# Last two chunks of a chunked mLSTM: products in a bank of their own, scores moved up, output work in two parts

## The chip, the cores and the metric

One NeuronCore of a Trainium2 chip runs the whole program. The metric is device time in microseconds (us), the median of several executions; a profiled execution gives the trace. The engines are TensorE (PE, with its weight loads PEld), VectorE (DVE), ScalarE (ACT), GpSimd (POOL) and SyncE (SP, which issues transfers). PE writes its results to PSUM, which has eight banks; DVE and ACT read them there.

## What is computed

An mLSTM layer (4 batches, 8 heads, 768 steps, head size 40), then a soft mixture of 8 experts and a second mixture with 8 Sinkhorn iterations, all on 3072 rows of 320. The part that matters here is the mLSTM:

```python
C = f_stab * C + i_stab * outer(v_t, k_t)
n = f_stab * n + i_stab * k_t
h_tilde = C @ q_t
denom = max(abs(n . q_t), 1)
y_t = sigmoid(o_t) * h_tilde / denom
```

## The kernel before

The mLSTM is done in chunks of 128 steps, six for each batch, 24 in all (numbers 0 to 23). For a chunk i the kernel makes:

- **scores** (`s_p`, L401): products of the transposed k and q, all heads, into two banks of the pool `ps_s`, which has two in all. `s_d` (L408, DVE, two instructions W0 and W1) multiplies them by the decay matrix `dd` in place, and with that frees the banks.
- **state** (`st_p`, L413, into bank `ob`; `st_d`, L429): the state after this chunk.
- **own products** (`pv`, L439): weighted scores times v, 32 small matmuls into the columns `o_in` of bank `oa`.
- **state products** (`p_st`, L449): q times the state before the chunk, 16 small matmuls, half into the columns `o_st` of `oa`, half into `ob`.
- **output** (`y_d`, DVE): two L460 read `o_st` and scale it into `u`, L467 adds `o_in`, L470, L474 and L475 make the denominator, L477 multiplies by the output gate. `y_g` (L487) multiplies by 1/denominator, on POOL, for chunk 23 on DVE.

Two chunks behind, `x_p`/`x_a` transpose the output rows (L498, copied by ACT at L503), and for each group of four chunks `lg_p` (L521) makes logits, `lg_d` (L529, L534, DVE) their running maximum, `lg_e` (ACT) the exponentials, `lt_p` (L562) transposes them, `sl_p` (L593) and `sl_d` (L604, DVE, accumulator `sacc`) sum the slot inputs.

`step(i)` writes the work of one iteration out in the order of the string `ORDER`; the last two chunks (22 and 23) use `ORDER_L`. PE, ACT and SP keep the order written, for the last two steps DVE does too; instructions of different hand-ordered blocks can still be interleaved on DVE and ACT by the scheduler that builds the program. In `ORDER_L` the score step `S` of iteration i makes the scores of chunk i+1. So PE's order at the end is: state 22, own products 22, state products 22, scores 23, logits of group 4, transposes of chunk 20, own products 23, state products 23, `lt_p`, transposes of chunk 21.

Then the string `TAIL` (L890) finishes the attention: transposes of chunks 22 and 23 (`x22p`, `x23p`), slot sums of group 4 (`s4p`, `s4d`), the transposed combine weights of groups 0 to 3 (`0p` to `3p`, `c_p`, L798, with `0a`.. on ACT and `0d`.. on DVE), logits of the last group (`lp`, `ld`), the maximum over all (`mxp`, L841), `wk` (two 512-column matmuls of the identity into bank `oa`, whose results nobody reads), and `ftp`/`ftd` (L868, L878), which end in `siT`, the slot inputs. `siT` feeds `up(0)` (L924), the first of the eight experts of the first mixture. The second mixture (L1184 to L1222) follows. The weights of the first mixture are fetched by SP during the attention and while its experts run.

Of the kernel before, what the change touches and what calls it, by code (L numbers as in the profile page):

```python
# [9 lines left out]
F32 = mybir.dt.float32  # L10
# [5 lines left out]
ALU = mybir.AluOpType  # L16
# [5 lines left out]
def mlstm_moe_kernel(  # L22
# [16 lines left out]
    nc = tc.nc  # L39
    B, H, S, D = q.shape  # L40
    N, DM = out.shape
    E, _, F = m2_w1.shape
    NS = phi.shape[1]
    SPE = NS // E
    BH = B * H
    P = 128
    L = 128
    NCH = S // L
    NT = N // P
# [6 lines left out]
    D1 = D + 1  # L56
# [6 lines left out]
    NXR = 13  # L63
    NBIG = 3
    ORDER = "LF' PK STm R DV DK O KT KTa ST STd E0 E0a E0g V I Y QT QTa Yg S W0 W1 E1 E1a E1g LP LV X Xa LD G LA W SM IR"
    ORDER_L = "LF' PK STm R DV DK O ST STd V I S W0 W1 Y Yg LP LV X Xa LD G LA W"
    PB = [1, 2, 3]
    PD = 3
    MAN2 = "Activation SP".split()
# [52 lines left out]
    ps_e = actx.enter_context(tc.tile_pool(name="ps_e", bufs=PB[0], space=PSUM))  # L122
    ps_s = actx.enter_context(tc.tile_pool(name="ps_s", bufs=PB[1], space=PSUM))
# [1 line left out]
    ps_o = actx.enter_context(tc.tile_pool(name="ps_o", bufs=1, space=PSUM))  # L125

    oa, ob = (ps_o.tile([P, 512], F32, name=n) for n in ("oa", "ob"))
    o_in = oa[:, 0:H * D1].rearrange("p (h d) -> p h d", h=H)
    o_st = [t[:, H * D1:H * D1 + JP * D1].rearrange("p (j d) -> p j d", j=JP) for t in (oa, ob)]
    o_c = ob[:, 0:JP * D1].rearrange("p (j d) -> p j d", j=JP)  # L130

# [7 lines left out]
    def xs_(i, w=DM):  # L139
        return xr[:, i % NXR, 0:w]  # L140
# [208 lines left out]
    def k_p(i, a):  # L349

        pt = ps_t.tile([P, JP, L], F32, tag="t", name="ptk")
        for j in range(JP):
            nc.tensor.transpose(  # L353
                pt[:, j, :], kq[i % NQ][:, a, 2 * j:2 * j + 2, :].rearrange("p h d -> p (h d)"), ident,
            )
        tmp["k", a, i] = pt

    def k_a(i, a, eng=None):
        t = pre.tile([P, JP, L], F32, tag=f"T{a}", name=f"T{a}", bufs=2 + a)
        if eng is None:  # L360
            nc.scalar.copy(out=t, in_=tmp.pop(("k", a, i)))  # L361
        else:
            eng.tensor_copy(t, tmp.pop(("k", a, i)))
        Ts[i, a] = t

    dds = {}
# [11 lines left out]
    def e_a(i, hh):  # L378
        dd = pre.tile([P, 4, L], F32, tag="dd", name="dd", bufs=6)
        nc.scalar.activation(out=dd, in_=tmp.pop(("e", i, hh)), func=AF.Exp)  # L380
        dds[i, hh] = dd
# [51 lines left out]
    def pv(i):  # L433

        TH = L // 2
        for r in range(2):
            for j in range(JP):
                for a in range(2):
                    nc.tensor.matmul(  # L439
                        o_in[TH * a:TH * a + TH, 2 * j + r, :], dds[i, r][:, j, TH * a:TH * a + TH],  # L440
                        vz[i % NV][:, 2 * j + r, :], start=True, stop=True, tile_position=(0, TH * a),
                    )

# [7 lines left out]
                    start=True, stop=True, tile_position=(DP * r, 0),  # L451
                )

    def y_d(i):
        b, c = divmod(i, NCH)
        src = o_in
        if c:
            src = mid.tile([P, H, D1], F32, tag="u", name="u", bufs=1)
            for r in range(2):
                nc.vector.tensor_tensor(  # L460
                    out=src.rearrange("p (j r) d -> p r j d", r=2)[:, r], in0=o_st[r],
                    in1=eGt[:, c, b * H:(b + 1) * H].rearrange("p (j r) -> p r j", r=2)[:, r].unsqueeze(2).to_broadcast(
                        [P, JP, D1]
                    ),
                    op=ALU.mult,
                )
            nc.vector.tensor_tensor(out=src, in0=src, in1=o_in, op=ALU.add)  # L467
        nq = mid.tile([P, H, 1], F32, tag="nq", name="nq")

        nc.vector.tensor_scalar(  # L470
            out=nq.bitcast(I32), in0=src[:, :, D:D1].bitcast(I32), scalar1=0x7FFFFFFF, scalar2=None,
            op0=ALU.bitwise_and,
        )
        nc.vector.tensor_scalar(out=nq, in0=nq, scalar1=1.0, scalar2=2.0, op0=ALU.max, op1=ALU.mult)  # L474
        nc.vector.reciprocal(nq, nq)  # L475
        xs = xs_(i).rearrange("p (h d) -> p h d", h=H)
        nc.vector.scalar_tensor_tensor(  # L477
            out=xs, in0=xs, scalar=1.0, in1=src[:, :, 0:D], op0=ALU.add, op1=ALU.mult,
        )
        nqs[i] = nq  # L480
# [3 lines left out]
    def y_g(i):  # L484
        xs = xs_(i).rearrange("p (h d) -> p h d", h=H)
        eng = nc.gpsimd if i < NT - 1 else nc.vector
        eng.tensor_tensor(out=xs, in0=xs, in1=nqs.pop(i).to_broadcast([P, H, D]), op=ALU.mult)  # L487
# [161 lines left out]

    ahead_parts = ahead()  # L650

    def step(i):
        b, c = divmod(i, NCH)
        n, s1 = i + 2, i + 1
        T, S1 = n < NT, s1 < NT
        X = i >= 2
        gq, j = divmod(i - 2, 4)
        gq -= 1
        if gq < 0 or not X:
            j = 9  # L660
        C_ = c < NCH - 1
        nxt = b + 1 < B

        ops = dict(
            KT=lambda: T and k_p(n, 0), KTa=lambda: T and k_a(n, 0),
            QT=lambda: T and k_p(n, 1), QTa=lambda: T and k_a(n, 1),
            E0=lambda: T and e_p(n, 0), E0a=lambda: T and e_a(n, 0), E0g=lambda: T and e_g(n, 0),
            E1=lambda: T and e_p(n, 1), E1a=lambda: T and e_a(n, 1), E1g=lambda: T and e_g(n, 1),
            ST=lambda: C_ and st_p(i), STm=lambda: C_ and st_m(i), STd=lambda: C_ and st_d(i),
            S=lambda: S1 and s_p(s1), W0=lambda: S1 and s_d(s1, 0), W1=lambda: S1 and s_d(s1, 1),  # L670
            PK=lambda: T and pr_k(n),
            V=lambda: pv(i), I=lambda: c and p_st(i),
            X=lambda: X and x_p(i - 2), Xa=lambda: X and x_a(i - 2),
            Y=lambda: y_d(i), Yg=lambda: y_g(i),
            G=lambda: i in SIG and sig_o(*SIG[i]),
            IR=lambda: c in (1, 2) and nxt and init_R(b + 1, c - 1, nc.vector.tensor_copy),
            LP=lambda: j < 3 and (lg_p, lt_p, sl_p)[j](gq), LV=lambda: j == 1 and lt_v(gq),
            LD=lambda: j < 3 and (lg_d, lt_d, sl_d)[j](gq), LA=lambda: j < 2 and (lg_e, lt_a)[j](gq),
            LF=lambda: j == 1 and lt_f(gq),
            O=lambda: load_o(*LO[i]),  # L680
            R=lambda: i + 3 < NT and load_R(i + 3),
            W=lambda: load_w(islice(ahead_parts, WN[i])),
            SM=lambda: i == 2 and load_small(),
            DV=lambda: T and i and load_v(n),
            DK=lambda: i + 4 < NT and load_kq(i + 4),
        )
        for o in (ORDER if i < NT - 2 else ORDER_L).split():
            if o.endswith("'"):
                if last:
                    last[-1][o[:-1]]()  # L690
            elif i < NT:
                ops[o]()
        last[:] = [ops]

# [65 lines left out]
        step(i)  # L760
    man2d = tc.manual_schedule(engines={mybir.EngineType.DVE})
    man2d.__enter__()
    for i in range(NT - 2, NT + 1):
        step(i)
    man2d.__exit__(None, None, None)
    if man2:
        man2.__exit__(None, None, None)
# [64 lines left out]
                tile_position=(0, 64 * a),  # L832
            )

    cbk = [(ps_e, "e"), (ps_s, "s"), (ps_s, "s"), (oa, None)]
    rs = pb.tile([P, 1, NS], F32, name="rs", bufs=1)
    siT = pb.tile([P, 3, NS], F32, name="siT", bufs=1)

# [25 lines left out]
    def ft_p():  # L864
        ptf = ob

        pfs = ps_e.tile([P, 512], F32, tag="e", name="pfs")[:, 0:NS]
        nc.tensor.matmul(  # L868
            pfs, sacc[:, DM:DM + 1].to_broadcast([P, P]), foldw, start=True, stop=True,
        )  # L870
        fold_t(ptf, sacc, foldw)
        tmp["f"] = ptf, pfs
# [7 lines left out]
            op=ALU.mult,  # L880
        )

    wm = oa.rearrange("p (a l) -> p a l", a=4)

    def wk():

        for _ in range(2):
            nc.tensor.matmul(wm, ident16, ident16.unsqueeze(1).to_broadcast([P, 4, L]), start=True, stop=True)

    TAIL = "x22p x22a 0p s4p 0a x23p x23a s4d 1p 2p lp 1a wk ld la mxp ls tp mxd wk tv mbp 0d mbd mba sp lc fwd sd 3p ftp tq 1d te ftd 2a 3a 2d ltd lta ltf 3d"  # L890
    ops = dict(
        wk=wk, x22p=lambda: x_p(NT - 2), x22a=lambda: x_a(NT - 2), s4p=lambda: sl_p(gl - 1), s4d=lambda: sl_d(gl - 1),
        x23p=lambda: x_p(NT - 1), x23a=lambda: x_a(NT - 1), lp=lambda: lg_p(gl), ld=lambda: lg_d(gl),
        la=lambda: lg_a(gl, 1), lc=lambda: lg_a(gl, 0), ls=lambda: lg_s(gl),
        tp=lambda: lt_p(gl, (1,)), tq=lambda: lt_p(gl, (0,)), tv=lambda: lt_v(gl, 1), te=lambda: lt_v(gl, 0), mxp=mx_p, mxd=mx_d,
        mbp=mb_p, mbd=mb_d, mba=mb_a, fwd=fw_d, sp=lambda: sl_p(gl), sd=lambda: sl_d(gl), ftp=ft_p, ftd=ft_d,
        ltd=lambda: lt_d(gl), lta=lambda: lt_a(gl), ltf=lambda: lt_f(gl),
    )
# [6 lines left out]
    if man3:  # L905
        man3.__enter__()
    for o in TAIL.split():
        ops[o]()
# [444 lines left out]
    for n in range(1, NBLK):  # L1353
        e, tb = divmod(n, NB)
# [60 lines left out]
```

## Time and profile before

| | |
|---|---|
| median of 3 runs | 942.7 us (941.76 to 942.98) |
| profiled execution | 941.64 us |
| its span, first to last instruction | 939.9 us |
| mean granted PE clock | 0.998 of full speed |
| PE busy | 98% of the span |
| chain of work that ended last | PE 94%, DVE 4% |

The span is what the trace covers; 1.74 us of the execution lie around it. Attention fills the first 172 us or so, the first mixture ends near 207 us, the rest is the second mixture. A row of the timeline gives start, duration, engine, line, operation, output <- inputs and the count of merged instructions; behind it, in brackets, how long the engine had been idle and what released it.

### The profile page before, as it was taken

Reading aid. Unit: us, or ns where it says so; the run is one execution under the profiler, and the core shown is the slowest. Engines: PE = TensorE matmul, PEld = TensorE weight load, DVE = VectorE, ACT = ScalarE, POOL = GpSimd, SP = SyncE. Lnnn points to the kernel's source line nnn. Section 1 sums busy time; section 2 is a strip of 40 time slices with the busy share of each in tenths; the row PEclk is TensorE's granted clock in tenths of the full one; section 3 lists DMA queues with packets and bytes.
Section 4 is the critical chain, followed back from the end, with each engine's and each line's share of the span. In section 5 each row is a group of like instructions: output and inputs, shape, how many; then the busy total and the mean of one; then the engine's idle time right before and its main releaser. Section 6 shows DMA issues by size and latency. Waiting matters only on the chain.

```text
span 939.9 us, 18808 instructions
## 1 busy us (share of the span) xinstructions
PE 917.4 (98%) x7966; PEld 631.6 (67%) x7966; DVE 576.8 (61%) x1182; ACT 358.0 (38%) x699; POOL 85.8 (9%) x151
## 2 busy tenths in 40 slices
PE   5999999999999999999999999999999999999998
PEld 3888887436767666666666666666666666666665
DVE  6667677645889785664665557555745464545443
ACT  3555554335334334422442344243424242423221
POOL 3555453000000000000000000000000000000000
PEclk9999999999999999999999999999999999999999
DMA  9999999960011011010110001010100000000111
GB/s 204 159 159 191 195 179 278 335 195 1 1 57 32 26 57 56 26 32 1 57 56 1 30 28 57 1 57 1 57 2 1 1 1 1 1 1 33 46 43 50
DMA packets 129612, 63.65 MB, mean 68 GB/s; under 512 B 103544, under 2 KB 123288, under 8 KB 129528
## 3 DMA queue, kind: packets, MB, share of 16 engines
q1 hardware_dynamic: 128416, 61.87, 28.7%
q8 instruction: 62, 1.02, 0.5%
q10 hardware_dynamic: 1112, 0.59, 0.3%
q14 instruction: 22, 0.18, 0.1%
HBM read 58.07 MB, written 4.08 MB: 66 GB/s over the span
## 4 chain that ended last, share of the span: by engine, by line
PE 94%; DVE 4%; ACT 1%; issue 1%; POOL 0%; ACTq 0%; DVEq 0%; POOLq 0%
PE y L1207 22%; PE y L1206 22%; PE y L1205 22%; PE z L1184 9%; PE pss L401 3%; PE oa L439 3%; PE ptk L353 3%; PE oa L449 2%; PE pu L924 2%; PE pe L371 2%; PE ob L413 1%; PE pd L962 1%; PE pu L931 1%; PE ptx L498 1%; DVE hl L1188 1%
## 5 line engine op out<-in xcount | busy, mean ns | idle before, releaser
L1206 PE MATMUL y<-wx,hh 128*128 128x320 f16 x1344 | 401.6, 299 | 0.4 <-DVE wx L1042 0.4
L1205 PE MATMUL y<-wx,hh 128*128 128x320 f16 x1344 | 401.9, 299 | 0.0
L1207 PE MATMUL y<-wx,hl 128*128 128x320 f16 x1344 | 401.7, 299 | 0.0
L1187 ACT ACTIVATE hh<-z 128x512 f16<-128x512 f32 x384 | 209.3, 594 | 438.2 <-PE z L1184 437.7
L1188 DVE SCALAR_TENSOR_TENSOR hl<-z,hh 128x512 f16<-128x512 f32 x384 | 248.2, 684 | 52.8 <-ACT hh L1187 52.3
L1220 DVE SCALAR_TENSOR_TENSOR acc<-y,Ps,acc 128x320 f32<-128x320 f32 x168 | 92.3, 550 | 209.9 <-PE y L1207 209.5
L1205 PEld LDWEIGHTS <-hh 128*128 128x128 f16 x1536 | 150.3, 98 | 75.0 <-issue 2.0
L1206 PEld LDWEIGHTS <-hh 128*128 128x128 f16 x1536 | 150.2, 98 | 73.4
L1207 PEld LDWEIGHTS <-hl 128*128 128x128 f16 x1536 | 149.9, 98 | 61.1 <-DVE hl L1188 1.9
L1184 PE MATMUL z<-cst,sst 96*128 96x512 f16 x384 | 115.7, 379 | 2.2 <-DVE hl L1188 1.4
L1207 PE MATMUL y<-wh,hl 128*128 128x320 f16 x192 | 57.4, 299 | 0.3 <-DVE hl L1188 0.3
L1205 PE MATMUL y<-wh,hh 128*128 128x320 f16 x192 | 57.4, 299 | 0.0
L1206 PE MATMUL y<-wl,hh 128*128 128x320 f16 x192 | 57.3, 299 | 0.0
L1184 PEld LDWEIGHTS <-sst 96*128 96x128 f16 x384 | 37.2, 98 | 18.7 <-issue 2.9
L353 PE MATMUL ptk<-ident,kq 128*128 128x128 f32 x192 | 31.1, 289 | 9.3 <-POOL ident masks.py:199 9.3
L361 ACT COPY T<-ptk 128x512 f32<-128x512 f32 x46 | 26.9, 585 | 31.7 <-PE ptk L353 31.4
L380 ACT ACTIVATE dd<-pe 128x512 f32<-128x512 f32 x48 | 29.0, 604 | 23.8 <-PE pe L371 20.5
L408 DVE TENSOR_TENSOR dd<-pss,dd 128x512 f32<-128x512 f32 x48 | 30.2, 670 | 9.1 <-PE pss L401 9.1
L1011 POOL PARTITION_ALL_REDUCE mr<-mxs x8 | 2.9, 365 | 325.0 <-DVE mxs L1030 325.0
L385 POOL TENSOR_SCALAR_AFFINE_SELECT dd<-dd 128x512 f32<-128x512 f32 x48 | 32.2, 675 | 4.2 <-ACT dd L380 4.2
L1011 POOL PARTITION_ALL_REDUCE mr<-mx x8 | 3.0, 375 | 295.6 <-DVE mx L1000 277.8
L353 PEld LDWEIGHTS ptk<-ident,kq 128*128 128x128 f32 x192 | 22.5, 146 | 10.5 <-POOL ident masks.py:199 9.3
(236 smaller groups left out, 753.8 us busy)
## 6 DMA issues: line engine op xcount, KB each, us to landing
wa<-in_moe_w_dram SPq DMA_DIRECT2D x18, 512.0 KB
raw<-in_moe_w_dram SPq DMA_DIRECT2D x28, 320.0 KB
kq<-in_k_dram SPq DMA_DIRECT2D x24, 160.0 KB
kq<-in_q_dram SPq DMA_DIRECT2D x24, 160.0 KB
vz<-in_v_dram SPq DMA_DIRECT2D x24, 160.0 KB
xr<-in_o_gate_dram SPq DMA_DIRECT2D x24, 160.0 KB
wb<-in_moe_w_dram SPq DMA_DIRECT2D x6, 640.0 KB
out_dram<-acc SPq DMA_DIRECT2D x24, 160.0 KB
```

Of the source, the lines that this page charges most:

```text
L353: nc.tensor.transpose(pt[:, j, :], kq[i % NQ][:, a, 2 * j:2 * j + 2, :].rearrange("p h d -> p (h d)"), ident,)
L380: nc.scalar.activation(out=dd, in_=tmp.pop(("e", i, hh)), func=AF.Exp)
L385: nc.gpsimd.affine_select(out=dd, in_=dd, pattern=[[0, 4], [1, L]], compare_op=ALU.is_ge, fill=0.0, base=0, channel_multiplier=-1,)
L401: nc.tensor.matmul(ps[r][:, j, :], Ts[i, 0][rs_, j, :], Ts[i, 1][rs_, j, :], start=True, stop=True, tile_position=(DP * r, 0),)
L408: nc.vector.tensor_tensor(out=dds[i, r], in0=tmp["s", i][r], in1=dds[i, r], op=ALU.mult)
L1184: nc.tensor.matmul(z, Sst[e][:, kc * P:(kc + 1) * P], cst[:, tb * TB:(tb + 1) * TB], start=True, stop=True,)
L1187: nc.scalar.activation(out=hh[:, kc, :], in_=z, func=AF.Relu)
L1188: nc.vector.scalar_tensor_tensor(out=hl[:, kc, :], in0=z, scalar=0.0, in1=hh[:, kc, :], op0=ALU.max, op1=ALU.subtract)
L1205: nc.tensor.matmul(y, hh[:, kc, ts], wh[e][:, kc, :], start=(kc == 0), stop=False)
L1206: nc.tensor.matmul(y, hh[:, kc, ts], wl[e][:, kc, :], start=False, stop=False)
L1207: nc.tensor.matmul(y, hl[:, kc, ts], wh[e][:, kc, :], start=False, stop=(kc == KF - 1))
L1220: nc.vector.scalar_tensor_tensor(out=a, in0=y, scalar=Ps[:, i, e:e + 1], in1=a, op0=ALU.mult, op1=ALU.add)
```

## The change

The own products of chunk 23 go to a tile `oe` of the pool `ps_e` (one bank) in place of `oa`. `y_d` is cut into `y_u` (L460, L467) and `y_r` (the rest). The steps 22 and 23 are no longer run one after the other: a string `LAST` writes out both, `a` for step 22 and `b` for step 23. In it the scores of chunk 23 (`aS`) stand ahead of the own products of the chunk before (`aV`, counted from 0 as chunk 22), and the own products of chunk 23 (`bV`) ahead of the output work of chunk 22. In `TAIL`, `0p` moves behind `x23p`, `2p` moves behind `lp` into the place of the first of two `wk`, which goes. Group 0's transposed weights and group 3's swap banks (`oa` and `ps_e`), as do `pfs` and `wm`.

```diff
-    ORDER_L = "LF' PK STm R DV DK O ST STd V I S W0 W1 Y Yg LP LV X Xa LD G LA W"
+    LAST = "aSTm aW bW aST aSTd aS aV aI aW0 aW1 bV aYu aLP bI aYr aYg aLD aLA aX aXa bYu bLP bLV bX bXa bYr bYg bLD bLA bLF"
...
-    o_in = oa[:, 0:H * D1].rearrange("p (h d) -> p h d", h=H)
+    banks = {}
+
+    def o_in(i):
+
+        return banks.get(i, oa)[:, 0:H * D1].rearrange("p (h d) -> p h d", h=H)
+
...
-    def y_d(i):
+    us = {}
+
+    def y_u(i):
         b, c = divmod(i, NCH)
-        src = o_in
+        src = o_in(i)
...
-            nc.vector.tensor_tensor(out=src, in0=src, in1=o_in, op=ALU.add)
+            nc.vector.tensor_tensor(out=src, in0=src, in1=o_in(i), op=ALU.add)
+        us[i] = src
+
+    def y_r(i):
+        src = us.pop(i)
...
-            Y=lambda: y_d(i), Yg=lambda: y_g(i),
+            Y=lambda: (y_u(i), y_r(i)), Yu=lambda: y_u(i), Yr=lambda: y_r(i), Yg=lambda: y_g(i),
...
-    for i in range(NT - 2, NT + 1):
-        step(i)
+    banks[NT - 1] = ps_e.tile([P, 512], F32, tag="e", name="oe")
+    ends = dict(a=step_ops(NT - 2), b=step_ops(NT - 1))
+    for o in LAST.split():
+        ends[o[0]][o[1:]]()
...
-    cbk = [(ps_e, "e"), (ps_s, "s"), (ps_s, "s"), (oa, None)]
+    cbk = [(oa, None), (ps_s, "s"), (ps_s, "s"), (ps_e, "e")]
...
-        pfs = ps_e.tile([P, 512], F32, tag="e", name="pfs")[:, 0:NS]
+        pfs = oa[:, 0:NS]
...
-    wm = oa.rearrange("p (a l) -> p a l", a=4)
-
     def wk():
 
+        wm = ps_e.tile([P, 4, L], F32, tag="e", name="wm")
...
-    TAIL = "x22p x22a 0p s4p 0a x23p x23a s4d 1p 2p lp 1a wk ld la mxp ls tp mxd wk tv mbp 0d mbd mba sp lc fwd sd 3p ftp tq 1d te ftd 2a 3a 2d ltd lta ltf 3d"
+    TAIL = "x22p x22a s4p x23p x23a s4d 0p 1p 0a lp 1a 2p ld la mxp ls tp mxd wk tv mbp 0d mbd mba sp lc fwd sd 3p ftp tq 1d te ftd 2a 3a 2d ltd lta ltf 3d"
```

## Rows read from the trace of the kernel before

**Rows 1.** The page's first part: busy time and share of each engine.

```profile
PE 917.4 (98%) x7966; PEld 631.6 (67%) x7966; DVE 576.8 (61%) x1182; ACT 358.0 (38%) x699; POOL 85.8 (9%) x151
```

**Rows 2.** The chain that ended last, 156 to 163 us: start, us, what.

```profile
156.63 1.02 PE pss L401 x16
157.76 0.55 issue
158.31 0.68 DVE dd L408
158.99 0.48 DVE u L460 x2
159.49 0.51 DVE u L467
160.04 1.13 PE oa L439 x32
...
162.24 0.56 DVE u L460 x2
```

**Rows 3.** PE's timeline at the end of the attention.

```profile
153.94 0.67 PE L413 MATMUL ob<-vz,kp 128*64 128x41 f32 x16
154.43 1.18 PE L439 MATMUL oa<-vz,dd 128*64 128x41 f32 x32
155.54 0.30 PE L449 MATMUL oa<-C,T 64*128 64x41 f32 x1
...
156.46 1.14 PE L401 MATMUL pss<-T,T 64*128 64x128 f32 x16
157.53 0.86 PE L521 MATMUL pl<-xT,phi_sb 112*32 112x128 f32 x24
158.32 0.54 PE L498 MATMUL ptx<-ident,xr 128*112 128x128 f32 x3
160.04 1.13 PE L439 MATMUL oa<-vz,dd 128*64 128x41 f32 x32 [1.18 <-DVE u L467]
161.10 0.30 PE L449 MATMUL oa<-C,T 64*128 64x41 f32 x1
...
163.06 0.60 PE L798 MATMUL ptc<-ident,ct_all 128*32 128x128 f32 x4
...
167.12 0.61 PE L888 MATMUL oa<-ident 128*128 128x512 f16 x2
```

**Rows 4.** DVE's timeline of the same stretch.

```profile
153.65 1.25 DVE L408 TENSOR_TENSOR dd<-pss,dd 128x512 f32<-128x512 f32 x2
...
158.91 0.32 DVE L460 TENSOR_TENSOR u<-oa,eGt 128x164 f32<-128x164 f32 x1
...
161.24 0.21 DVE L534 TENSOR_SCALAR nmx<-gm,nmx 128x1 f32<-128x1 f32 x1
162.22 0.33 DVE L460 TENSOR_TENSOR u<-oa,eGt 128x164 f32<-128x164 f32 x1 [0.77 <-PE ob L449]
...
164.37 0.49 DVE L487 TENSOR_TENSOR xr<-xr,nq 128x320 f32<-128x320 f32 x1
...
164.98 0.54 DVE L604 SCALAR_TENSOR_TENSOR sacc<-sacc,sc,pq 128x321 f32<-128x321 f32 x1
```

**Rows 5.** PE's timeline: entry to the experts, and the second mixture's first weights.

```profile
172.41 1.07 PE L924 MATMUL pu<-wa,siT 128*32 128x256 f32 x16 [0.33 <-DVE siT L878]
...
202.63 1.07 PE L924 MATMUL pu<-big,soT 128*32 128x256 f32 x16
```

**Rows 6.** Busy time by stretch: stretch, length, engines (count), granted clock, DMA share, GB/s.

```profile
18.00:20.00 2.00, 0.42 (x2) 0.00 (x1) 0.82 (x4) 0.60 (x1) 0.69 (x2) 0.95 1.01 177
20.00:22.00 2.00, 2.00 (x15) 1.62 (x16) 0.00 (x0) 0.60 (x1) 1.38 (x3) 0.50 0.94 304
...
194.00:196.00 2.00, 2.00 (x30) 0.89 (x30) 0.66 (x2) 1.37 (x3) 0.00 (x0) 1.00 0.38 105
```

**Rows 7.** PE's timeline: scores while the clock was low.

```profile
20.38 2.08 PE L401 MATMUL pss<-T,T 64*128 64x128 f32 x16
```

More of the change, by code (lines that the diff above doesn't have):

```diff
@@ L435, in pv @@
         TH = L // 2
+        o = o_in(i)
         for r in range(2):
@@ L439, in pv @@
                     nc.tensor.matmul(
-                        o_in[TH * a:TH * a + TH, 2 * j + r, :], dds[i, r][:, j, TH * a:TH * a + TH],
+                        o[TH * a:TH * a + TH, 2 * j + r, :], dds[i, r][:, j, TH * a:TH * a + TH],
                         vz[i % NV][:, 2 * j + r, :], start=True, stop=True, tile_position=(0, TH * a),
@@ L650, in mlstm_moe_kernel, with step_ops @@
     ahead_parts = ahead()
-    def step(i):
+    def step_ops(i):
         b, c = divmod(i, NCH)
@@ L662, in step @@
         nxt = b + 1 < B
-        ops = dict(
+        return dict(
             KT=lambda: T and k_p(n, 0), KTa=lambda: T and k_a(n, 0),
@@ L686, in step @@
         )
-        for o in (ORDER if i < NT - 2 else ORDER_L).split():
+    def step(i):
+        ops = step_ops(i)
+        for o in ORDER.split():
             if o.endswith("'"):
@@ L690, in step @@
                     last[-1][o[:-1]]()
-            elif i < NT:
+            else:
                 ops[o]()
```

## The prediction

> **What bounds the kernel now.** I read the page's busy shares first: PE is busy for 98% of the span and DVE for 61% [rows 1], so time can only be won where PE stands still or where its order makes something else late. The change touches only the end of the attention, so next came the chain of waits from 156 to 163 us [rows 2]. The reader is to see that there the chain leaves PE: scores of chunk 23, a hand-over, the second of the two L408 on them, the output work L460 and L467 of chunk 22 on DVE, and only then PE again with the own products of chunk 23. PE's timeline shows the price: before those products, at 160.04, PE had stood idle for 1.18 us, released by L467 [rows 3]. The cause is the bank: L467 of chunk 22 reads from `oa` what the own products of chunk 23 would overwrite, and on DVE it stands behind L408 of chunk 23, which waited for scores that PE made after both products of chunk 22. DVE's timeline shows the other end: L460 of chunk 23 starts at 162.22, released by the state products [rows 4]. From there to the first expert at 172.41, which waits for `siT` [rows 5], the work follows chunk 23's output, so I measure the change by when that L460 starts.
>
> **The order of PE, step by step.** The new order is state 22, scores 23, own products 22, state products 22, own products 23, logits of group 4, state products 23. I take for each the distance between starts in the old order.
>
> The scores come forward into a new wait. They need both banks of `ps_s`, and the second is free when W1 of chunk 22 ends: the two L408 run from 153.65 for 1.25 us, to 154.90 [rows 4]. Before, PE could go on at 154.43 [rows 3]; now it stands until about 154.95, with 0.05 us for the release (L467 ended at 159.49 + 0.51 = 160.00 and PE started at 160.04 [rows 2]). This costs 0.52 us, and every product behind it in PE's queue pays it.
>
> From there, by the starts in [rows 3]: scores 1.07 (156.46 to 157.53), so own products 22 at 156.02; those 1.11 (154.43 to 155.54), so state products 22 at 157.13; those 0.92 (155.54 to 156.46), so own products 23 at 158.05. Their weighted scores are ready: the scores end near 156.1, and two L408 of 1.25 us bring that to 157.4. Own products 23 take 1.06 (160.04 to 161.10), so logits at 159.11. The logits take 0.79 us (157.53 to 158.32), so state products 23 at 159.90. From the start of state products to L460 it took 1.12 (161.10 to 162.22 [rows 3, 4]), so L460 of chunk 23 starts at **161.02 in place of 162.22: 1.20 us earlier**. That is the 1.18 us of idle and the 0.55 us and more of hand-over that no longer stand between, less the 0.52 us of the new wait and the logits that now run inside the stretch.
>
> **Does DVE keep up?** Output work of chunk 22 starts at 157.13 + 1.12 = 158.25. From L460 to the end of L534 it was 158.91 to 161.45, 2.54 us [rows 4], so DVE is through at 160.79, ahead of 161.02 by 0.23 us. Cutting the output work in two adds no instruction; on DVE nothing comes between the two parts, so it costs nothing. If DVE was the later one, the gain would end at 1.43 us.
>
> **The bank.** `p_st` of chunk 23 still writes to `oa`, while L467 of chunk 22 reads other columns of it. By address it waits only for L460, by bank for L467 too. L467 ends 1.09 us after the first L460 starts (158.91 to 160.00), at 159.34, so PE's 159.90 holds either way. At the very worst, with L467 of chunk 22 no earlier than now, state products 23 could start at 160.04 in place of 161.10, and the gain were still 1.06 us. In the Trainium skill the page PSUM — Partial Sum Buffer, section "PSUM bank collisions raise a hardware error", asks for a guard by bank and not by address, which speaks against winning a full step with one spare bank; by that rule the sum lies between 1.06 and 1.20 us. No row here shows it by itself, since the old own products write the very columns that L467 reads.
>
> **The tail.** Moving `0p` behind `x23p` keeps two `c_p` between `x23p` and the logits of the last group, as `1p` and `2p` were. `2p` takes the place of a filler: 0.60 us of transposes (the row at 163.06) for 0.61 us of filler (at 167.12) [rows 3]. Its cover is PE's wait for the maximum; without that cover it would cost its 0.60 us. The swap of banks only exchanges two users that come in the same order. On SP the weight fetches of steps 22 and 23 keep their order, and no other transfer is moved; on POOL there is no new instruction. So the tail moves up as a block by 1.20 us, and `siT` with it.
>
> **Behind it.** The experts start when `siT` is there [rows 5]. Their weights must be there as well: the transfers are busy until the stretch 194 to 196, where the share falls to 0.38 [rows 6], and the last of that batch to be used, the first weights of the second mixture, are read at 202.63 [rows 5], some 7 us later. So the rest moves up too. The second mixture is PE throughout.
>
> **The sum:** 1.20 us from 941.64 gives 940.44 for an execution like the profiled one. That one lies 1.06 us under the median of the runs, so the forecast for the median is 942.7 - 1.2 = **941.5**. About 0.2% (1.9 us) is what a measurement of this kernel can tell from no change: I forecast a real gain that is under it.
>
> **Rivals.**
>
> *The slot sum cuts in.* `s4p` no longer has `0p` ahead of it, so it ends earlier against chunk 23's output, and L604 can be put ahead of L487 on DVE; before, it came right behind (164.98 after 164.37 [rows 4]). For: the old order already has it between instructions of another block. Against: `s4p` waits for exponentials that wait for L534, and L534 ends only 0.66 us earlier (161.45 to 160.79), while L487 moves by 1.20. It takes 0.45 to 0.54 us: gain 0.70, time 942.0.
>
> *The experts don't follow.* If a load is the real bound of the expert stage, the 1.2 us turn into a wait there: 942.7. For: the transfers are saturated up to 194 us [rows 6]. Against: the 7 us of room above.
>
> *More than that.* DVE's bound gives 1.43 us, and if PE's wait for W1 were shorter and small gaps closed as well, 1.9 or more: 940.7. Against: PE's own work between 155 and 161 us is all still there.
>
> *The clock falls, and it gets slower.* A filler is gone, and the granted clock fell once before: in 18 to 20 PE was busy for only 0.42 of 2 us, and in 20 to 22 the clock was 0.50, the level of 1.2 GHz [rows 6]; sixteen score products then took 2.08 us [rows 7] in place of 1.14 [rows 3]. The place would be the hand-overs of the tail, from which it would last into the experts. It costs half of the time that PE's bound work spends at the lower level: 2.4 us of it eat the gain, and from 6.2 us on (a cost of 3.1, the gain and 1.9) the kernel is slower by over 0.2%: 944.6 and above. Against: PE's idle of 1.18 us disappears and only idle of about 0.5 us comes, and the old tail with both kept 1.00. The Trainium skill (TensorE: Matmul & The Clock Gate, section "HAM oscillation — how this bites in real kernels") warns that an engine that waits between bursts starts the next one at the lower clock; the stretch from 18 to 22 us agrees, and by that rule a tail with less to do for PE is the risk of this change.
>
> **How the numbers follow.** Forecast (941.5) 0.64; slot sum 0.15; experts don't follow 0.08; more 0.07; clock 0.06. Forecast, slot sum and the unmoved experts lie between 941 and 942.7; the runs of before spread by 0.9 us below and 0.3 above their median, so the range is 940.4 to 942.9, leaving out the two outer cases. Faster by over 0.2% (below 940.8): the 0.07 and 0.02 of the forecast's lower edge, 0.09. Slower by over 0.2% (above 944.6): 0.04 of the clock's 0.06. Within: 0.87.
>
> **What would show it.** In the new trace PE runs the own products of chunk 23 without idle ahead of them, the scores of chunk 23 start at 154.95 after a wait for L408, L460 of chunk 23 starts near 161.0, the first expert near 171.2, and everything behind it keeps its length. I am wrong if own products or state products of chunk 23 wait for L467, if L604 stands ahead of L487, if the clock leaves 1.00 after 160 us, or if the first expert moves up and the second mixture doesn't.

## The result: slower by 0.65%, and the profile after

The changed kernel took 950.7 us, the kernel before 942.7 us in the same session; the ratio is 1.0065 with a 95% interval of 1.0043 to 1.0088. I had forecast 941.5 us, with 0.04 for slower by over 0.2%. One of its five executions, the profiled one, took 1193.4 us at a mean granted clock of 0.752 and is left out of the ratio, though not of the median; the other four took 946.8 to 951.6 us. The rows below are of a later execution of the same kernel (the run `e4_after_again`), which took 946.42 us with a span of 944.7.

Lines of the changed kernel are numbered a little higher: own products L445, state products L455, output work L468 and L475, L499 for the last factor, L825 for the VectorE step of the combine weights, L895 for `siT`, L940 for the first expert's products.

PE's timeline of the changed kernel at the end of the attention answers to [rows 3, 5]:

```profile
154.88 0.67 PE L418 MATMUL ob<-vz,kp 128*64 128x41 f32 x16
155.47 1.57 PE L406 MATMUL pss<-T,T 64*128 64x128 f32 x16
156.97 1.13 PE L445 MATMUL oa<-vz,dd 128*64 128x41 f32 x32
...
159.05 1.13 PE L445 MATMUL oe<-vz,dd 128*64 128x41 f32 x32
160.11 0.86 PE L533 MATMUL pl<-xT,phi_sb 112*32 112x128 f32 x24
160.91 0.30 PE L455 MATMUL oa<-C,T 64*128 64x41 f32 x1
...
164.81 0.51 PE L510 MATMUL ptx<-ident,xr 128*112 128x128 f32 x3 [0.44 <-DVE xr L499]
...
169.79 0.61 PE L815 MATMUL ptc<-ident,ct_all 128*32 128x128 f32 x4
...
176.25 1.94 PE L940 MATMUL pu<-wa,siT 128*32 128x256 f32 x16 [4.37 <-DVE cst L825]
178.12 1.04 PE L947 MATMUL pu<-wa,siT 64*32 64x256 f32 x8
...
180.05 1.07 PE L940 MATMUL pu<-big,siT 128*32 128x256 f32 x16
```

Up to 165 us this is the forecast: the own products of chunk 23 go to `oe` with no idle ahead of them. The surprise is the first expert (L940 on `wa`): PE stands idle for 4.37 us ahead of it, and what releases it is not `siT` but L825. VectorE's timeline of the same execution answers to [rows 4]:

```profile
159.15 0.33 DVE L468 TENSOR_TENSOR u<-oa,eGt 128x164 f32<-128x164 f32 x1 [0.93 <-PE ob L455]
...
161.50 0.21 DVE L546 TENSOR_SCALAR nmx<-gm,nmx 128x1 f32<-128x1 f32 x1
162.03 0.33 DVE L468 TENSOR_TENSOR u<-oa,eGt 128x164 f32<-128x164 f32 x1 [0.32 <-PE ob L455]
...
171.90 0.26 DVE L895 TENSOR_TENSOR siT<-ob,rs 128x96 f32<-128x96 f32 x1
172.70 0.68 DVE L825 SCALAR_TENSOR_TENSOR cst<-ptc,cst 32x512 f16<-32x512 f32 x1 [0.54 <-ACT cst L819]
...
175.43 0.68 DVE L825 SCALAR_TENSOR_TENSOR cst<-ptc,cst 32x512 f16<-32x512 f32 x1
```

`siT` is done at 172.16. The last L825 ends at 176.11: that is `3d`, the last VectorE step of the tail, which reads group 3's transposes (the PE row at 169.79; before they went to `oa`, now they go to the bank of `ps_e`). The chain of waits tells the same, from the L825 ahead of it (`2d`) on, with the row sums of the last group between the two:

```profile
172.70 0.68 DVE cst L825
...
175.43 0.69 DVE cst L825
176.12 0.14 issue
176.25 1.94 PE pu L940 x16
```

And the clock falls in that idle. Busy time by stretch (stretch, length, busy time of the engines with counts, granted clock, DMA share, GB/s):

```profile
172.00:174.00 2.00, 0.00 (x0) 0.00 (x0) 1.41 (x4) 1.15 (x3) 0.00 (x0) 1.00 1.01 312
174.00:176.00 2.00, 0.00 (x0) 0.00 (x0) 1.51 (x6) 0.31 (x1) 0.00 (x0) 0.90 1.07 243
176.00:178.00 2.00, 1.75 (x16) 0.68 (x16) 1.97 (x4) 0.00 (x0) 0.00 (x0) 0.50 1.06 350
178.00:180.00 2.00, 1.48 (x14) 0.40 (x10) 1.14 (x2) 0.38 (x1) 0.39 (x1) 0.75 0.31 111
```

At 0.50, the 1.2 GHz level, the first expert's sixteen products take 1.94 us; the second's, at full clock, 1.07.

Executions differ at their very start, so I compare from one point in the tail: the start of the state products of chunk 22 (L413 before, L418 after), at 153.94 us before and 154.88 here. From there to the first expert it was 172.41 - 153.94 = 18.47 us before [rows 3, 5] and is 176.25 - 154.88 = 21.37 now; to the end of the span 939.9 - 153.94 = 785.96 and 944.7 - 154.88 = 789.82. So in this execution 2.90 us are lost by the time the first expert starts and 0.96 more behind it.

### The profile page after: what moved, and what is told of

It reads as the page before. It is cut to its first block, busy times and chain, and to the rows that moved or that the text cites. A ratio compares the mean times of both kernels' runs of the same rounds, so it can differ in the third digit from the quotient of the medians.

```text
span 1191.7 us, 18805 instructions
## 1 busy us (share of the span) xinstructions
PE 1171.0 (98%) x7964; PEld 722.5 (61%) x7964; DVE 577.0 (48%) x1182; ACT 359.5 (30%) x699; POOL 83.7 (7%) x151
## 4 chain that ended last, share of the span: by engine, by line
PE 97%; DVE 1%; ACT 0%; issue 0%; ACTq 0%; POOL 0%; DVEq 0%
PE y L1223 23%; PE y L1221 23%; PE y L1222 23%; PE z L1200 9%; PE pss L406 3%; PE ptk L358 3%; PE oa L445 2%; PE oa L455 2%; PE pu L940 2%; PE pe L376 1%; PE ob L418 1%; PE pd L978 1%; PE pu L947 1%; PE ptx L510 1%; PE ob L291 1%; PE pl L533 0%
## 5 line engine op out<-in xcount | busy, mean ns | idle before, releaser
L1221 PE MATMUL y<-wx,hh 128*128 128x320 f16 x1344 | 477.7, 355 | 0.0
L1222 PE MATMUL y<-wx,hh 128*128 128x320 f16 x1344 | 476.1, 354 | 0.0
L1223 PE MATMUL y<-wx,hl 128*128 128x320 f16 x1344 | 475.6, 354 | 0.0
L1222 PEld LDWEIGHTS <-hh 128*128 128x128 f16 x1536 | 172.1, 112 | 119.9 <-issue 31.9
L1221 PEld LDWEIGHTS <-hh 128*128 128x128 f16 x1536 | 171.3, 112 | 119.6 <-issue 29.3
L1223 PEld LDWEIGHTS <-hl 128*128 128x128 f16 x1536 | 171.4, 112 | 101.3 <-DVE hl L1204 0.6
L1200 PE MATMUL z<-cst,sst 96*128 96x512 f16 x384 | 143.1, 460 | 0.3 <-DVE sst L1137 0.3
L1223 PE MATMUL y<-wh,hl 128*128 128x320 f16 x192 | 68.3, 356 | 0.2 <-DVE hl L1204 0.2
L1222 PE MATMUL y<-wl,hh 128*128 128x320 f16 x192 | 68.0, 354 | 0.0
L1221 PE MATMUL y<-wh,hh 128*128 128x320 f16 x192 | 67.5, 351 | 0.0
L413 DVE TENSOR_TENSOR dd<-pss,dd 128x512 f32<-128x512 f32 x48 | 30.9, 685 | 9.7 <-PE pss L406 8.9
L406 PE MATMUL pss<-T,T 64*128 64x128 f32 x384 | 33.8, 322 | 0.0
L406 PEld LDWEIGHTS pss<-T,T 64*128 64x128 f32 x384 | 28.8, 223 | 7.4 <-issue 7.4
```

Of the source, the lines that this page charges most:

```text
L406: nc.tensor.matmul(ps[r][:, j, :], Ts[i, 0][rs_, j, :], Ts[i, 1][rs_, j, :], start=True, stop=True, tile_position=(DP * r, 0),)
L413: nc.vector.tensor_tensor(out=dds[i, r], in0=tmp["s", i][r], in1=dds[i, r], op=ALU.mult)
L1200: nc.tensor.matmul(z, Sst[e][:, kc * P:(kc + 1) * P], cst[:, tb * TB:(tb + 1) * TB], start=True, stop=True,)
L1221: nc.tensor.matmul(y, hh[:, kc, ts], wh[e][:, kc, :], start=(kc == 0), stop=False)
L1222: nc.tensor.matmul(y, hh[:, kc, ts], wl[e][:, kc, :], start=False, stop=False)
L1223: nc.tensor.matmul(y, hl[:, kc, ts], wh[e][:, kc, :], start=False, stop=(kc == KF - 1))
```

## The experiments

The theory after this reading, "bank": when the attention's PSUM pools close, the experts' pools are opened over the same banks. The first of them, `psz`, gives its first tile to the first expert, and the first bank is the one that `ps_e`, the first pool of the attention, had. So the first expert waits for the last reader of `ps_e`. Before, that was `ftd`, which ends in `siT`; now it is `3d`, the last step of all. Rivals: the missing filler lets the clock fall; the new order costs by itself.

**1. The tail's banks as before.** Edit to the changed kernel:

```diff
-    cbk = [(oa, None), (ps_s, "s"), (ps_s, "s"), (ps_e, "e")]
+    cbk = [(ps_e, "e"), (ps_s, "s"), (ps_s, "s"), (oa, None)]
-        pfs = oa[:, 0:NS]
+        pfs = ps_e.tile([P, 512], F32, tag="e", name="pfs")[:, 0:NS]
-        wm = ps_e.tile([P, 4, L], F32, tag="e", name="wm")
+        wm = oa.rearrange("p (a l) -> p a l", a=4)
```

> The changed kernel with the bank swap of the tail alone taken back (group 0's transposes and pfs in the ps_e bank, group 3's and the fillers in oa). Theory 'bank': the first expert's products get the PSUM bank that ps_e had, and in the changed kernel they wait there for the last reader of group 3's transposes, the last VectorE step of the tail; with the swap back that wait goes and the 1.2 us of the forecast stay: 941.5 us, first expert 0.1 us behind siT, mean clock 0.998. Theory 'filler': the clock falls because one filler is gone, and the wait is beside the point: stays at 950 us, clock 0.99. Theory 'order': the scores ahead of the own products cost time themselves: above 943 us.

Measured: 942.08 us beside 943.52 before, ratio 0.9991 (0.9977 to 1.0005). PE's timeline:

```profile
155.62 0.67 PE L418 MATMUL ob<-vz,kp 128*64 128x41 f32 x16
...
165.55 0.51 PE L510 MATMUL ptx<-ident,xr 128*112 128x128 f32 x3 [0.44 <-DVE xr L499]
...
172.95 1.07 PE L940 MATMUL pu<-wa,siT 128*32 128x256 f32 x16 [0.33 <-DVE siT L895]
```

The wait is gone: the first expert follows `siT` again, 17.33 us behind the reference point, 1.14 less than before, and the end comes 784.78 us behind it, 1.18 less. That is the gain that I had forecast, with everything of the change but the swap; it is read from the trace, for the ratio by itself does not tell it from no change. I had expected a mean clock of 0.998; five of the twelve executions had 0.991 to 0.993 (see experiment 7).

**2. The swap alone, on the kernel before.** The same three edits the other way round, order and fillers untouched.

> The kernel before with the bank swap of the tail alone; both fillers stay. 'Bank': the first expert waits for the last VectorE step of group 3, which ended at 176.3 us before, while the expert started at 172.4: 4 us of idle, and if the clock falls in it up to 5 us more: 946.7 to 952 us. 'Filler' and 'order': 942.7 us, nothing changes.

Measured: 951.86 us, ratio 1.0090 (1.0070 to 1.0109). PE's timeline, then the stretches:

```profile
154.79 0.67 PE L413 MATMUL ob<-vz,kp 128*64 128x41 f32 x16
...
177.29 1.94 PE L924 MATMUL pu<-wa,siT 128*32 128x256 f32 x16 [4.37 <-DVE cst L808]
```

```profile
174.00:176.00 2.00, 0.00 (x0) 0.00 (x0) 1.51 (x6) 0.49 (x2) 0.00 (x0) 0.90 1.08 275
176.00:178.00 2.00, 0.71 (x8) 0.46 (x12) 1.92 (x5) 0.00 (x0) 0.00 (x0) 0.50 1.01 326
...
184.00:186.00 2.00, 2.00 (x20) 0.59 (x16) 0.00 (x0) 0.38 (x1) 0.00 (x0) 0.54 0.70 236
```

The same 4.37 us of idle, released by the same step. The first expert is 22.50 us behind the reference point, 4.03 later than before, and the end 7.35 later: the 4.03 us are the 2.90 that the changed kernel loses there and the 1.14 that it gains with the swap taken back. The clock falls with both fillers in place, so it needs no missing filler.

**3. `3d` earlier.** In the changed kernel the last step moves ahead of `2d` and of the row sums:

```diff
-... 2a 3a 2d ltd lta ltf 3d"
+... 2a 3a 3d 2d ltd lta ltf"
```

> The changed kernel with group 3's last VectorE step moved ahead of group 2's and of the row sums, banks as changed. 'Bank': the wait of the first expert shrinks from 4.3 us to about 1.9 us and the clock need not fall: 943.4 us, up to 947 if it falls. 'Filler' and 'order': as the changed kernel, 950 us.

Measured: 944.56 us, ratio 1.0011 (0.9997 to 1.0025). VectorE's timeline, PE's, then the stretches:

```profile
173.07 1.28 DVE L825 SCALAR_TENSOR_TENSOR cst<-ptc,cst 32x512 f16<-32x512 f32 x2 [1.02 <-ACT cst L819]
```

```profile
154.78 0.67 PE L418 MATMUL ob<-vz,kp 128*64 128x41 f32 x16
...
173.90 1.07 PE L940 MATMUL pu<-wa,siT 128*32 128x256 f32 x16 [2.12 <-DVE cst L825]
```

```profile
172.00:174.00 2.00, 0.10 (x4) 0.13 (x8) 0.98 (x3) 1.04 (x3) 0.00 (x0) 1.00 1.00 339
174.00:176.00 2.00, 1.54 (x24) 0.52 (x23) 1.49 (x6) 0.69 (x2) 0.00 (x0) 1.00 1.08 249
```

The idle is 2.12 us, the clock stays at 1.00 behind it, and the end is 786.32 us behind the reference point: 0.36 later than before. The first of the two merged L825 is now `3d`; the first expert starts before the second, `2d`, has ended at 174.35. So the wait follows the step that was named.

**4. The changed kernel once more**, for the trace shown above.

> The changed kernel once more, for a trace at full clock. 'Bank': PE idle for some 4 us ahead of the first expert, released by the last VectorE step of group 3, then a stretch at the lower clock level in the first expert's products; 947 to 952 us. 'Filler': the clock is below full level before that idle begins.

Measured: 947.73 us, ratio 1.0050 (1.0034 to 1.0067). Behind its start the clock is 1.00 until the idle and falls in it, as 'bank' has it.

**5. The experts' pools in the other order.** The changed kernel with its swap; only these two lines change places:

```diff
-    psz = ctx.enter_context(tc.tile_pool(name="psz", bufs=3, space=PSUM, reuse_waits="tile"))
     psy = ctx.enter_context(tc.tile_pool(name="psy", bufs=3, space=PSUM, reuse_waits="tile"))
+    psz = ctx.enter_context(tc.tile_pool(name="psz", bufs=3, space=PSUM, reuse_waits="tile"))
```

> The changed kernel with its bank swap, but the two PSUM pools of the experts are opened in the other order, so that the first expert's products lie in the banks that the pool of transposes had, not in the bank of group 3's. 'Bank': no wait for the last VectorE step of group 3, the first expert starts within 0.3 us of siT, 1.2 us less than before as in the first experiment (some 942 us beside 943.5 before). If the cause is anything else in the tail: as the changed kernel, 947 us or more.

Measured: 941.99 us beside 943.12 before, ratio 0.9976 (0.9959 to 0.9993). PE's timeline:

```profile
155.97 0.67 PE L418 MATMUL ob<-vz,kp 128*64 128x41 f32 x16
...
173.40 1.07 PE L940 MATMUL pu<-wa,siT 128*32 128x256 f32 x16 [0.42 <-ACT lt L580]
```

Group 3's transposes still lie in the bank of `ps_e` and `3d` is still last, but the first expert no longer waits for it: it starts 17.43 us behind the reference point, released by a copy out of the transposes' pool that ends near `siT`, and the end comes 784.83 us behind it, 1.13 less than before. So the wait comes from the bank that the first expert is given, and from nothing else in the tail. This version is the one whose ratio shows it faster than the kernel before.

**6 and 10. The wait filled.** Into the changed kernel, behind the last transposes of the tail, 18 matmuls of the identity into a tile of the transposes' pool. Experiment 10 is the same kernel again, in one session with experiment 9, the changed kernel.

```diff
+    def wf():
+        wt = ps_t.tile([P, 4, L], F32, tag="t", name="wt")
+        for _ in range(18):
+            nc.tensor.matmul(wt, ident16, ident16.unsqueeze(1).to_broadcast([P, 4, L]), start=True, stop=True)
-... ftp tq 1d te ftd 2a ...
+... ftp tq wf 1d te ftd 2a ...
```

> The changed kernel with 18 matmuls of the identity into a bank of the pool of transposes, which PE runs while it waits for the bank. 'Bank', with the clock as its second half: the first expert starts as late as in the changed kernel (some 2.8 us later than before), but the granted clock stays at 1.00 behind it, so the time is before + 2.8: 946.3 us, with no runs above 949. If the wait itself cost nothing and all were the clock: 942.3 us. If the clock were no part of it: as the changed kernel, 947.7 us and more.

> The changed kernel beside the next one on the same chip. Wait and clock together: before + 2.9 us of wait + 1 to 5 us at the lower clock, so before + 4 to 8.

> The kernel with the wait filled, beside the changed one on the same chip. If the lower clock behind the wait is the second part of the loss, this stays at before + 2.5 to 2.9 us and the difference to the changed kernel is what the clock costs, 1.5 us or more; if both are alike, the earlier difference came from the chips.

Measured: 945.64 us in experiment 6, ratio 1.0031 (1.0011 to 1.0050). Three of its ten executions took 948.3 to 950.1, at a mean clock of 0.991 to 0.993; I had expected none above 949, and two were. In experiments 9 and 10, on one chip, the changed kernel took 951.77 us, ratio 1.0074 (1.0052 to 1.0096), and the filled one 945.50, ratio 1.0029 (1.0012 to 1.0046), beside 943.11 before: 8.7 us lost where I had expected 4 to 8, and 2.4 where I had expected 2.5 to 2.9. PE's timeline of experiment 6 and its stretch behind the wait:

```profile
154.71 0.67 PE L418 MATMUL ob<-vz,kp 128*64 128x41 f32 x16
...
171.55 4.05 PE L910 MATMUL wt<-ident 128*128 128x512 f16 x18
176.08 1.07 PE L946 MATMUL pu<-wa,siT 128*32 128x256 f32 x16 [0.48 <-DVE cst L825]
```

```profile
176.00:180.00 4.00, 3.42 (x50) 1.42 (x50) 2.96 (x4) 0.76 (x2) 0.39 (x1) 1.00 1.04 313
```

The first expert starts exactly as late, 21.37 us behind the reference point, but at full clock: its products take 1.07 us. In experiment 9 it starts 21.37 us behind too, and the clock behind it stays low for longer than in experiment 4. This execution also had a low clock at its start, from 18 to 36 us, far ahead of the tail:

```profile
158.78 0.67 PE L418 MATMUL ob<-vz,kp 128*64 128x41 f32 x16
...
180.15 1.93 PE L940 MATMUL pu<-wa,siT 128*32 128x256 f32 x16 [4.37 <-DVE cst L825]
```

```profile
34.00:36.00 2.00, 2.00 (x19) 1.48 (x19) 1.29 (x2) 1.16 (x2) 0.69 (x2) 0.50 1.45 163
...
178.00:180.00 2.00, 0.00 (x0) 0.00 (x0) 1.60 (x5) 0.25 (x1) 0.00 (x0) 0.85 1.05 362
180.00:182.00 2.00, 1.85 (x16) 0.68 (x16) 1.97 (x4) 0.00 (x0) 0.00 (x0) 0.50 0.26 93
...
186.00:188.00 2.00, 2.00 (x20) 0.60 (x20) 0.00 (x0) 0.38 (x1) 0.00 (x0) 0.50 1.04 390
188.00:190.00 2.00, 2.00 (x17) 0.73 (x10) 0.48 (x1) 0.00 (x0) 0.00 (x0) 0.59 0.08 19
```

So the loss has two parts: the wait, 945.50 - 943.11 = 2.4 us by the medians (2.53 by the traces, end to reference point, 788.49 in experiment 6 against 785.96), and what the filling takes away, the low clock behind the wait. The medians put 951.77 - 945.50 = 6.3 us on this second part, but not all of that is shown to be it. In the traces the end of experiment 9 (span 951.4) comes 951.4 - 158.78 = 792.62 us behind the reference point, 4.13 more than in experiment 6; in experiment 4 it is 789.82, 1.33 more. Experiment 9's reference point itself comes 4.84 us later than the 153.94 of the kernel before, and that part lies ahead of the changed order and goes with the low clock at its start. How much of the 6.3 us is of either kind in the executions without a trace stays open.

**7. The filler back.** Experiment 1's kernel, with group 0's transposes in PE's gap ahead of `x23p`, `2p` ahead of the logits again and the first filler in its old place:

```diff
-    TAIL = "x22p x22a s4p x23p x23a s4d 0p 1p 0a lp 1a 2p ld ...
+    TAIL = "x22p x22a s4p 0p x23p x23a 0a s4d 1p 2p lp 1a wk ld ...
```

> The first experiment's kernel (old banks) with the first filler back in its place: group 0's transposes go into PE's gap ahead of chunk 23's transposes, group 2's stand ahead of the logits again. 'Filler': of the 12 executions of the first experiment 5 had a mean clock of 0.991 to 0.993 and took 944 to 945.6 us, of the kernel before 1 of 23 so low; with the filler back these become rare and the median falls to 941.3. If that low clock has nothing to do with the filler: the same mix, median 942.

Measured: 941.73 us, ratio 0.9986 (0.9970 to 1.0003). Two of its 12 executions had a mean clock of 0.991 and took 945.6 and 946.6 us, but 7 of 35 of the kernel before, run beside it, had 0.991 to 0.993 and took 945.8 to 947.7, and of experiment 5, which has one filler fewer, none of 10: the filler makes no difference that these runs show. Experiment 1 was not run beside this one, so why 5 of its 12 executions were so low stays open. Experiment 8, by chance, has the profile of such an execution (mean clock 0.993), and there the clock is low at the start of the kernel, long before the tail, and 1.00 all through the tail:

```profile
20.00:22.00 2.00, 1.57 (x11) 1.06 (x12) 0.00 (x0) 0.97 (x2) 0.93 (x2) 0.52 0.93 267
...
28.00:30.00 2.00, 2.00 (x26) 1.41 (x25) 0.33 (x1) 0.88 (x2) 0.30 (x1) 0.50 0.80 137
```

The kernel before is back at 1.00 by 24 to 26 us in the execution profiled ahead of the prediction. In this trace of experiment 7 the first expert is 172.42 - 154.66 = 17.76 us behind the reference point, so these moves together cost 0.43 us of the gain. The timeline shows where, at VectorE's step L596:

```profile
154.66 0.67 PE L418 MATMUL ob<-vz,kp 128*64 128x41 f32 x16
...
166.33 0.28 DVE L596 TENSOR_REDUCE sm<-ct_all 128x4 f32<-128x128 f32 x1 [0.90 <-ACT ct_all L591]
...
172.42 1.07 PE L940 MATMUL pu<-wa,siT 128*32 128x256 f32 x16 [0.33 <-DVE siT L895]
```

It waits 0.90 us for ScalarE's L591, where it waited 0.43 us in experiment 1: the copy `0a` (L819, 0.58 us), which moved up with `0p`, now stands ahead of L591.

**8. The order alone.** Experiment 1's kernel without the bank of its own; the logits fill PE's wait for the output work of chunk 22:

```diff
-    LAST = "... aST aSTd aS aV aI aW0 aW1 bV aYu aLP bI ...
+    LAST = "... aST aSTd aS aV aI aW0 aW1 aYu aLP bV bI ...
-    banks[NT - 1] = ps_e.tile([P, 512], F32, tag="e", name="oe")
```

> Old banks in the tail, and no bank of its own for chunk 23's products: only the scores are moved up, and the logits of group 4 fill PE's wait for the output work of chunk 22. By the steps of the prediction that wait is back: the own products of chunk 23 start some 1.3 us later, behind the logits only 0.5 us later, so of the 1.2 us gain 0.5 go and 0.7 stay: 942.8 us beside 943.5 before. If the bank of its own is what counts: no gain at all, 943.5.

Measured: 944.47 us, ratio 1.0004 (0.9985 to 1.0023): inconclusive by time. By its trace PE waits 0.38 us for L475 ahead of the own products of chunk 23, and L468 of chunk 23 starts 0.45 us later behind the reference point (158.07 here) than in experiment 4, near the 0.5 us that I had expected. But something else eats the rest. PE's timeline, then VectorE's:

```profile
163.49 1.13 PE L445 MATMUL oa<-vz,dd 128*64 128x41 f32 x32 [0.38 <-DVE u L475]
```

```profile
167.33 0.45 DVE L489 SCALAR_TENSOR_TENSOR xr<-xr,u 128x320 f32<-128x320 f32 x1
168.16 0.55 DVE L616 SCALAR_TENSOR_TENSOR sacc<-sacc,sc,pq 128x321 f32<-128x321 f32 x1 [0.38 <-PE pq L605]
168.63 0.48 DVE L499 TENSOR_TENSOR xr<-xr,nq 128x320 f32<-128x320 f32 x1
```

Here the slot sum L616 stands ahead of L499: VectorE waits 0.38 us for PE and then works on it, while the output of chunk 23 stands behind. This is my rival "the slot sum cuts in", in a kernel that was not predicted. The end comes 944.2 - 158.07 = 786.13 us behind the reference point, 0.17 later than before. So what the order is worth without the bank stays open: the one build that was tried lost its gain to another step.

## Why the prediction was wrong, step by step

Times below are behind the start of the state products of chunk 22, the forecast's from 153.94, the changed kernel's from 154.88.

- **The order of PE: right.** Own products 22 forecast at 2.08, measured 2.09; own products 23 at 4.11 and 4.17; logits 5.17 and 5.23; state products 23 5.96 and 6.03; L460 of chunk 23 at 7.08 and 7.15 (L468), against 8.28 before. The gain there is 1.13 us where I had said 1.20. The new wait for the banks of `ps_s` has another form than forecast: the scores start at 0.59, not 1.01, and wait inside their row, 1.57 us in place of 1.14; the own products behind them start when I had said. My sentence on what the 1.20 us consist of was wrong, though the sum of starts was right: the logits stand in the stretch before and after, and the 0.55 us of hand-over pass while PE makes them. What leaves the stretch is the idle, 1.18, and the transposes of chunk 20, 0.54; what comes in is the 0.52 of the new wait.
- **VectorE keeps up: right.** L546 ends at 6.83 (forecast 6.85), and L468 of chunk 23 is released by PE's state products 0.32 us later.
- **The bank rule inside the attention: no wait.** L475 of chunk 22 ends at 160.25, PE starts the state products of chunk 23 at 160.91. So whether a guard must go by bank, as the Trainium skill has it (PSUM — Partial Sum Buffer, "PSUM bank collisions raise a hardware error"), or by address, no run here shows: the wait would have been over either way. The first expert does not show it either, since its products overwrite columns that `3d` reads.
- **The tail as a block: right as far as `siT`**, which ends 17.28 us behind the reference point against 18.42 (172.36 before), 1.14 us earlier. That is the 1.13 us that L468 of chunk 23 had gained, so the moves of `0p` and `2p` cost nothing that the trace shows.
- **"The swap of banks only exchanges two users that come in the same order": the step that failed.** I followed the swap's users within the attention and put it at zero. Its other half is the next owner of the bank. The first expert was 21.37 us behind the reference point in place of 17.33 with the swap taken back: the term that I had put at nothing was 4.04 us of wait. With the idle filled and the clock kept at 1.00 (experiment 6), the end still comes 788.49 - 784.78 = 3.71 us later than with the swap taken back (experiment 1). Experiments 1, 2, 3 and 5 each move this wait by itself.
- **"So the rest moves up too": wrong for the same reason.** The weights were not the cause, as I had argued; the wait names L825.
- **The rival "the clock falls"** had the place (from the tail into the experts), the price (nearly half of the time spent at the lower level: 1.94 us for products that take 1.07) and the sign, but not the cause. I tied it to the missing filler; it needed the 4.37 us of idle. The 0.06 that I gave it was small because I did not ask what could lengthen PE's idle between tail and experts. The Trainium skill's warning (TensorE: Matmul & The Clock Gate, "HAM oscillation — how this bites in real kernels") holds here: the burst behind the idle starts at the lower clock in experiments 2, 4 and 9, and not where the idle is filled or shorter.
- **The slot sum**: it stayed behind L499 in the changed kernel, as forecast.

## What to carry to other kernels

When two users swap memory, look at who owns each piece next, past the end of the stage: a pool that is opened over a closed one inherits its last reader. Do not let the last step of a stage read the bank that the next stage's first product is given. And a wait of PE can cost twice: once as idle, and once more in what runs behind it at the lower clock. Here 4.37 us of idle did that, 2.12 us did not; and once the idle was filled with matmuls, only the wait itself was left to pay. Compare traces from a point inside them, too: the start of an execution moved by more than this change is worth.

## What was not expected of the hardware

How long the clock stays low behind the same idle differs much between executions. After 4.37 us of idle the stretch was back at 1.00 by 180 to 182 us in experiment 4, 0.96 us lost by the end of the span; in experiment 9 it was still at 0.50 at 186 to 188, and in experiment 2 at 0.54 at 184 to 186, with 3.3 us lost behind the first expert (7.35 less 4.03); in experiment 9 it was 3.76 (792.62 less 785.96, less 2.90). The wait itself does not differ: the first expert starts 21.37 us behind the reference point in every trace of the changed kernel shown here. That the low clock behind the wait is all that spreads the kernel's medians from 947.7 to 951.8 us is not shown, for the start of an execution differs as well: the clock was back at 1.00 by 26 us in experiment 4, and in experiment 9 it was still at 0.50 at 34 to 36 us, and their reference points lie 3.90 us apart. The idle of 2.12 us in experiment 3 left the clock at 1.00. Why one execution comes back sooner than another, at its start or behind the wait, was not tried.
